# A spectral layer beside softmax attention on one core: two chunks projected together, values stored as rows, the spectral part in two halves of the sequence, seven more buffer pairs and runs of 13 key tiles

## The chip, the core and the metric

The kernel runs on one core of one Trainium2 chip. A core has a matrix engine (TensorE, "PE" in the profile, its weight loads "PEld"), VectorE ("DVE"), ScalarE ("ACT"), GpSimd ("POOL") and SyncE ("SP"), which here issues nearly all DMAs. The on-chip memory SBUF has 128 partitions; matrix products land in PSUM, which has eight banks of 128 x 512 numbers. The metric is the device time of one execution in microseconds (us), the median of several runs.

## What is computed

Two layers work on two inputs of 2048 rows and 448 columns, and their results stand side by side in the output (2048 x 896):

```python
# A: Fourier mixing, the real part alone
a = x @ dft_hid_re.T                        # 2048 x 448
b = x @ dft_hid_im.T
y = dft_seq_re @ a - dft_seq_im @ b         # 2048 x 2048 times 2048 x 448, twice

# B: attention with 16 heads of 28 columns
q, k, v = split(x @ wqkv)
p = softmax(q @ k.T * 28 ** -0.5)           # 2048 x 2048 per head
out = concat_heads(p @ v) @ wo
```

All inputs are 32-bit floats. To keep that precision on TensorE's faster 32-bit format, the kernel splits each factor of the projections and of the spectral part into a high and a low part and multiplies high x high, low x high and high x low. A contraction over 448 rows is 3 x 3 + 2 = 11 matmuls (the last 64 rows hold both parts at once).

## The kernel before, in words

**Stages on TensorE.** The q and k projections (a weight block j of 128 columns, a chunk c of 512 positions, 11 matmuls of 128 x 512 each; seven blocks, four chunks), the values (16 tiles of 128 positions, 11 matmuls of 128 x 448), the spectral part, attention, and the output projection (16 tiles, L1003). Two kinds of work are interleaved over almost the whole span: *attention* (scores, L865, and products with the values, L848) and *fill* (everything else, L581 and L718), which TensorE does between scores, while ScalarE computes exponentials.

**The planner.** The program's instructions are not written in the order in which they run. Each operation is added to `Schedule` with its engine, a *key* (the time at which it is due), an estimated duration, what it depends on, and the buffers that it takes. `Schedule.run` plays the program through with these estimates: when an engine is free it issues the ready operation with the smallest key whose buffers can be had. The order so found is fixed for each engine in the program; the chip then only waits for semaphores. SyncE is one queue, with at most eight DMAs outstanding (`LANES`), whose speed is estimated by `FLOW_IN` in the first 20 us and by `FLOW` later. Fill matmuls form one chain (`last`), each after the one before it; scores form another.

**The head.** The first three weight blocks come as four DMAs of 192 KB (rows k = 0 to 3, L559), x as sixteen of 256 KB (chunk c, rows k, L488). ScalarE writes the high part (L490 for x, L560 for weights), VectorE (L427) or GpSimd (L562) the low one. `first_chunk` takes chunk 0 alone: for each k, three steps (high x high, low weight, low x) of three matmuls each (L616), into three banks. The other chunks go through `project`, 11 matmuls in a row (L581), with two banks in turn (`fill_s`, `NFILL` = 2; the other six banks are `bank_s`). A result goes out through `stored`: ScalarE copies the high part (L597), VectorE subtracts the low part (L598), both are stored to DRAM (L600, L601). `warm` issues `N_WARM` matmuls on a tile of ones before the data are there (L920).

**The values.** A tile of 128 positions is copied to 16 groups of 32 columns (28 of data, a one for the sum, zeros) and stored to `v_d`, laid out head, partition, position tile and column (L675). `head_loads` fetches one head's part for all positions (L773), keyed four planned microseconds before the head begins; two such buffers exist.

**The spectral part.** `hidden(part)` makes a (part 0) or -b (part 1) for all 16 position tiles in `big`, where x lay before, so it waits for the last projection (`x_users`). `sequence(part)` then makes 16 output tiles: four pieces of the sequence matrix for each (a DMA of 256 KB, L523, split by ScalarE, L524, and GpSimd, L530), 12 matmuls per piece (L718), 48 in one bank. In part 0, VectorE copies the result out and it is stored to `y_d` (L732, L733). In part 1, the stored tile is loaded again once piece `Q_YO` has begun (L735), added (L736) and written to the output (L738).

**Attention.** Head h has keys from `begins[h]` = 56 + h x 54.94 us on. `scores` issues for each of its 16 key tiles four matmuls (128 x 512) and four exponentials into two pairs. A *pair* is a buffer of `kept_s`: 128 x 2 x 512 numbers, of which there are `NKEPT` = 22; three more are lent where the memory `wd` is not holding weights. `quad` multiplies a key tile's exponentials by the values: four matmuls that each use 32 columns of the array, side by side. TensorE does such quads in runs: `sums` groups consecutive key tiles, and a run waits for all its exponentials. Its length is taken by `run_size` from the planned time of its first tile: 8 below 230 us, 10 from there on. The planner prices each passage from scores to a run at `PE_TURN`.

**The end.** After a head's last quad, `out_of` fetches the sums, inverts and spreads them by three rounds of DMA, multiplies (GpSimd, L910) and stores the head's output to `on_d`. The output projection reads it in four chunks n, splits it (ScalarE L985; the subtraction on GpSimd for n < `OUT_DVE`, on VectorE from there on), multiplies (L1003) and writes the output (L1011). A flag that sums and values are within bounds decides whether `any_scores`, a slow general path, runs behind; with these inputs it does not.

Of the kernel before, what the change touches and what calls it, by code (L numbers as in the profile page):

```python
# [11 lines left out]
F32 = mybir.dt.float32  # L12
# [8 lines left out]
S = 2048  # L21
# [15 lines left out]
Q_YO = 2  # L37
N_WARM = 7
N_FIRST = 3
RUN_AT = ((0.0, 8), (230.0, 10))  # L40
# [9 lines left out]
OUT_DVE = 2  # L50
# [17 lines left out]
FLOW, FLOW_IN = 200.0, 310.0  # L68
# [264 lines left out]
def tile_kernel(ctx, tc, xa, wre, wim, wd, xb, wqkv, wo, out):  # L333
# [18 lines left out]
    v_d = dram.tile([H, P, NT * VW], F32, name="vd")  # L352
# [5 lines left out]
    big = new("big", [P, 2 * NT * D], F32R)  # L358
# [20 lines left out]
    kept_s.lent = lent  # L379
    fill_s, bank_s = Slots(banks[:NFILL]), Slots(banks[NFILL:])  # L380
# [80 lines left out]

    def x_h(k, s):
        return big[:, k * S + s.start:k * S + s.stop]

    def x_l(k, s):
        return big[:, (3 + k) * S + s.start:(3 + k) * S + s.stop]

    def x_3(s):
        return big[:, 6 * S + s.start:6 * S + s.stop]

    ab_h = big[:, :NT * D].rearrange("p (t d) -> p t d", t=NT)
    ab_l = big[:, NT * D:].rearrange("p (t d) -> p t d", t=NT)
# [113 lines left out]
    def lz(f, *a):  # L586
        return lambda: f(*a)
# [15 lines left out]
    def first_chunk(w):  # L603

        cols = slice(0, CH)
        os = [(bank_s if j else fill_s).slot() for j in range(N_FIRST)]
        pairs = [kept_s.slot() for _ in range(N_FIRST)]
        end = {}
        for k in range(4):
            for step in ((0, 0, 0), (1, 0, 1), (0, 1, 2))[:3 if k < 3 else 2]:  # L610
                wl, xl, n = step
                for j in range(N_FIRST):
                    x = lz(x_3, cols) if k == 3 else lz(x_l if xl else x_h, k, cols)

                    def emit(e, j=j, k=k, n=n, wl=wl, x=x):
                        nc.tensor.matmul(os[j].t, w.part(j, k, wl)(), x(), start=(k == 0 and n == 0), stop=(k == 3 and n == 1))  # L616
                    ready = [*(w.los[k] if wl else w.his[k]), xb_ready[0, k] if xl or k == 3 else xb_hi[0, k]]
                    done = k == 3 and n == 1
                    last[0] = pe(fkey(1, M512), emit, d=M512, deps=[last[0], *ready],
                                 use=[*w.own, os[j], *([pairs[j]] if done else ())])  # L620
                    if done:
                        end[j] = last[0]
# [301 lines left out]
    for c in range(NC):  # L924
        load_x(c, 0.2 + 3 * c)
# [206 lines left out]
```

## Time and profile before

| What | Value |
|---|---|
| median of 3 runs | 1010.89 us (1010.7 to 1011.0) |
| the profiled execution | 1010.71 us, of which the span of the trace 1008.9 us |
| TensorE | 1001.6 us busy, 5634 matmuls |
| its weight loads | 735.3 us |
| ScalarE | 712.3 us |
| GpSimd | 366.9 us |
| VectorE | 319.8 us |
| DMA | 124.84 MB, 109908 packets, 48640 of them under 512 B |
| first matmul on data | 5.28 us from the start of the span |
| granted TensorE clock | 1.000 on average |

The profile's rows give an engine, a line of the kernel, what is written and read (buffer numbers left out), shapes and times. In rows in order of time, the first column is the start, the second the length, "x3" the number of instructions in the group, and the bracket the idle time before it with what ended it. A matmul's length is its passage through the array; consecutive ones overlap, so what one costs is the distance from start to start. The quads appear with two records per matmul, so a run of 8 key tiles has 64 records.

### The profile page before, as it was taken

Reading aid. Unit: us, or ns where it says so; the run is one execution under the profiler, and the core shown is the slowest. Engines: PE = TensorE matmul, PEld = TensorE weight load, DVE = VectorE, ACT = ScalarE, POOL = GpSimd, SP = SyncE. Lnnn points to the kernel's source line nnn. Section 1 sums busy time; section 2 is a strip of 40 time slices with the busy share of each in tenths; the row PEclk is TensorE's granted clock in tenths of the full one; section 3 lists DMA queues with packets and bytes.
Section 4 is the critical chain, followed back from the end, with each engine's and each line's share of the span. In section 5 each row is a group of like instructions: output and inputs, shape, how many; then the busy total and the mean of one; then the engine's idle time right before and its main releaser. Section 6 shows DMA issues by size and latency. Waiting matters only on the chain.

```text
span 1008.9 us, 15993 instructions
## 1 busy us (share of the span) xinstructions
PE 1001.6 (99%) x5634; PEld 735.3 (73%) x5634; DVE 319.8 (32%) x608; ACT 712.3 (71%) x1410; POOL 366.9 (36%) x338
## 2 busy tenths in 40 slices
PE   8999999999999999999999999999999999999998
PEld 7896667777766876686668667766786677667797
DVE  6362525251515042412314051614042152300112
ACT  6117979788767866796679778877786687668242
POOL 5112234353324323442325443434334252444530
PEclk9999999999999999999999999999999999999999
DMA  9797464323233333333233424332433343233463
GB/s 327 226 163 205 127 188 150 98 76 114 69 102 102 112 96 106 97 106 102 80 111 110 132 71 119 93 112 80 148 98 100 117 141 105 70 123 117 139 187 130
DMA packets 109908, 124.84 MB, mean 124 GB/s; under 512 B 48640, under 2 KB 61440, under 8 KB 109824
## 3 DMA queue, kind: packets, MB, share of 16 engines
q1 hardware_dynamic: 109824, 123.78, 40.8%
q8 instruction: 45, 0.74, 0.3%
q14 instruction: 39, 0.32, 0.1%
HBM read 89.92 MB, written 33.69 MB: 123 GB/s over the span
## 4 chain that ended last, share of the span: by engine, by line
PE 98%; DVE 1%; DMA 1%; SPq 0%; issue 0%; DVEq 0%
PE bank L718 31%; PE bank L865 23%; PE bank L848 22%; PE bank L581 17%; PE bank L1003 4%; PE bank L806 1%; DMA kept<-xb 1%; DVE big L427 0%; SPq L488 0%; SPq L559 0%; DVE kept L598 0%; DVE kept L736 0%; DVEq L427 0%
## 5 line engine op out<-in xcount | busy, mean ns | idle before, releaser
L869 ACT ACTIVATE kept<-bank 128x512 f32<-128x512 f32 x944 | 509.4, 673 | 90.7 <-PE bank L865 87.6
L530 POOL TENSOR_TENSOR wlo<-wraw,whi 128x512 fp32r<-128x512 f32 (+1 forms) x164 | 202.9, 1237 | 471.4 <-ACT whi L524 397.1
L865 PE MATMUL bank<-q,k 98*128 98x512 f32 x960 | 329.4, 398 | 0.0
L718 PE MATMUL bank<-big,whi 128*128 128x448 f32 x1024 | 310.9, 367 | 0.0
L848 PE MATMUL bank<-kept,v 128*32 128x512 f32 x2016 | 224.4, 593 | 0.0
L718 PEld LDWEIGHTS bank<-big,whi 128*128 128x128 f32 x1024 | 193.3, 189 | 29.2 <-issue 3.4
L865 PEld LDWEIGHTS bank<-q,k 98*128 98x128 f32 x960 | 180.4, 188 | 44.2 <-issue 11.7
L718 PE MATMUL bank<-big,wlo 128*128 128x448 f32 x512 | 188.3, 368 | 0.0
L848 PEld LDWEIGHTS bank<-kept,v 128*32 128x32 f32 x2016 | 63.5, 110 | 144.4 <-issue 142.3
L524 ACT ACTIVATE whi<-wraw 128x512 fp32r<-128x512 f32 x164 | 113.8, 694 | 21.0 <-PE bank L718 17.0
L718 PEld LDWEIGHTS bank<-big,wlo 128*128 128x128 f32 x512 | 96.7, 189 | 16.9 <-issue 5.9
L837 POOL TENSOR_TENSOR kept<-kept,mb 128x512 f32<-128x512 f32 x54 | 79.5, 1473 | 62.9 <-DVE mb L832 27.5
L581 PE MATMUL bank<-wd,whi 128*128 128x448 f32 x256 | 79.8, 367 | 0.0
L811 DVE STREAM_TRANSPOSE mb<-bank 128x512 f32<-128x512 f32 x64 | 45.8, 715 | 101.6 <-PE bank L806 87.9
L839 ACT ACTIVATE kept<-kept 128x512 f32<-128x512 f32 x64 | 45.1, 772 | 33.3 <-POOL kept L837 29.9
L581 PE MATMUL bank<-big,whi 128*128 128x512 f32 x175 | 60.1, 394 | 0.2 <-DVE kept L598 0.2
L832 DVE STREAM_TRANSPOSE mb<-am 128x512 f32<-128x512 f32 x64 | 45.4, 710 | 41.1 <-POOL kept L837 39.9
L810 ACT ACTIVATE kept<-bank 128x512 f32<-128x512 f32 x64 | 41.6, 672 | 22.5 <-PE bank L806 21.6
L581 PEld LDWEIGHTS bank<-wd,whi 128*128 128x128 f32 x256 | 48.3, 189 | 6.1 <-issue 0.8
L894 ACT ACTIVATE kept<-bank 128x512 f32<-128x512 f32 x16 | 9.5, 597 | 55.1 <-PE bank L848 55.1
L776 DVE TENSOR_REDUCE ok<-v 128x1 f32<-128x512 f32 x16 | 11.0, 686 | 115.5 <-DMA v<-vd 115.4
L736 DVE TENSOR_TENSOR kept<-bank,kept 128x448 f32<-128x448 f32 x15 | 9.3, 623 | 120.2 <-PE bank L718 106.0
(74 smaller groups left out, 745.8 us busy)
## 6 DMA issues: line engine op xcount, KB each, us to landing
wraw<-wre SPq DMA_DIRECT2D x64, 256.0 KB
wraw<-wim SPq DMA_DIRECT2D x64, 256.0 KB
qkd<-kept SPq DMA_DIRECT2D x40, 256.0 KB
wraw<-xa SPq DMA_DIRECT2D x32, 256.0 KB
k<-qkd SPq DMA_DIRECT2D x64, 112.0 KB
q<-qkd SPq DMA_DIRECT2D x64, 112.0 KB
out<-kept SPq DMA_DIRECT2D x31, 224.0 KB
kept<-xb SPq DMA_DIRECT2D x16, 256.0 KB
```

The lines of the kernel that those rows point to most:

```text
L524: a = act(key + (0 if early else 1), lambda: nc.scalar.activation(self.hi.t, raw.t, AF.Copy), ACT_S, soon=SOON, deps=[ld], acq=[self.hi], ...
L530: b = sch.add(e, at, lambda g: eng[g].tensor_tensor(self.lo.t[:, :n], raw.t[:, :n], f32(self.hi.t)[:, :n], op=ALU.subtract), deps=[a], acq ...
L581: nc.tensor.matmul(o.t[:, :cols], w(), x(), start=(i == 0), stop=(i == n - 1))
L718: nc.tensor.matmul(o.t[:, :D], a.t[:, k, :], b[:, q * 4 + k, :], start=(q == 0 and k == 0 and j == 0), stop=(q == 3 and k == 3 and j == 2))
L810: made.append(act(key, lambda o=o, s=s: nc.scalar.activation(s.t, o.t, AF.Copy), deps=[m], use=[o, s.pair], lock=[o]))
L811: t = dve(key, lambda o=o, tm=tm: nc.vector.transpose(tm.t, o.t), 0.73, deps=[m], acq=[tm], use=[o], lock=[o], own=RAW_S)
L832: t = dve(key, lambda mb=mb, c=c: nc.vector.transpose(mb.t, f32(am.t)[:, c * NT:(c + 1) * NT].unsqueeze(2).to_broadcast([P, NT, 32])), 0.7 ...
L837: sh = sch.add({"DVE": 0.8, "POOL": POOL_2}, key, lambda e, s=s, mb=mb: eng[e].tensor_tensor(s.t, s.t, mb.t, op=ALU.add), deps=[t, made[c] ...
L839: shown.append(act(key, lambda s=s: nc.scalar.activation(s.t, s.t, AF.Exp, scale=SCALE), ACT_S, deps=[sh], use=[s.pair]))
L848: nc.tensor.matmul(o.t[c * VW:(c + 1) * VW, :], VT[h].t[:, kt // 4, kt % 4, :], tiles[c].t, start=(kt == 0), stop=(kt == NT - 1))
L865: m = pe(key, lambda e, o=o, q=q, kt=kt: nc.tensor.matmul(o.t, KT[h][kt // 4].t[:KM, kt % 4 * P:(kt % 4 + 1) * P], q.t[:KM, :], start=True ...
L869: es[h, kt].append(act(key - 20, lambda o=o, p=p: nc.scalar.activation(p.t, o.t, AF.Exp, scale=SCALE), deps=[m], use=[o, p.pair]))
```

## The change

Six things change together.

- **Two chunks together.** `first_chunks` takes chunks 0 and 1: for each k it does the nine matmuls of chunk 0, then those of chunk 1, into six banks. x for chunk 1 is now requested between that of chunk 0 and the next weights. Two more warm-up matmuls are issued; the planner's time for the warm-up stays as it was.
- **Values as rows.** `v_d` is laid out partition, position tile, head and column: a tile's store is one contiguous row per partition, a head's load is 16 pieces of 32 numbers per partition.
- **x in two sides.** x lies in two tiles of half the sequence each. The first later takes a and b; the second is given up after the last projection (`held`) and serves as seven more pairs.
- **The spectral part in two halves of the sequence.** `hidden` and `sequence` run four times, for part 0 and 1 and the two halves; a pass sums eight position tiles, 24 matmuls per bank. The first pass stores its tiles, the next two load, add and store them, the last loads, adds and writes the output. The hidden weights are loaded again for each pass, into the memory that is otherwise lent.
- **Runs of 13.** A run has 8 key tiles below 200 planned us and 13 from there on.
- **Smaller settings.** `FLOW` is 225 (was 200), `OUT_DVE` 1 (was 2), `Q_YO` 1 (was 2, of then four pieces, now two).

```diff
-Q_YO = 2
-N_WARM = 7
+Q_YO = 1
+N_WARM = 9
-RUN_AT = ((0.0, 8), (230.0, 10))
+RUN_AT = ((0.0, 8), (200.0, 13))
-OUT_DVE = 2
+OUT_DVE = 1
-FLOW, FLOW_IN = 200.0, 310.0
+FLOW, FLOW_IN = 225.0, 310.0
...
-    v_d = dram.tile([H, P, NT * VW], F32, name="vd")
+    v_d = dram.tile([P, NT, H * VW], F32, name="vd")
...
-    big = new("big", [P, 2 * NT * D], F32R)
+    SIDE = 7 * S // 2
+    xs = [new(f"x{i}", [P, SIDE], F32R) for i in range(2)]
...
+    more, N_MORE = [], SIDE // (2 * CH)
+    def place_of(i):
+        if not more:
+            more.append(sb.tile([P, N_MORE, 2, CH], F32, tag="x1", name="more"))
+        return more[0][:, i]
+    held = [Slot(kept_s) for _ in range(N_MORE)]
+    for i, slot in enumerate(held):
+        slot.i = len(kept_s.tiles)
+        kept_s.tiles.append(lambda i=i: place_of(i))
...
-    def first_chunk(w):
+    def first_chunks(w, chunks):
+        os = {(c, j): (bank_s if j else fill_s).slot() for c in chunks for j in range(N_FIRST)}
+        pairs = {cj: kept_s.slot() for cj in os}
         end = {}
         for k in range(4):
+            for c in chunks:
+                for wl, xl, n in ((0, 0, 0), (1, 0, 1), (0, 1, 2))[:3 if k < 3 else 2]:
+                    for j in range(N_FIRST):
...
-                v_done[c].append(dma(key - 20, lambda vs=vs, c=c, t=t: nc.sync.dma_start(
-                    v_d[:, :, (4 * c + t) * VW:(4 * c + t + 1) * VW].rearrange("h p x -> p h x"),
-                    vs.t.rearrange("p (h x) -> p h x", h=H)), extra=1.0, deps=[b], use=[pair]))
+                v_done[c].append(dma(key - 20, lambda vs=vs, c=c, t=t: nc.sync.dma_start(v_d[:, 4 * c + t, :], vs.t),
+                                     deps=[b], use=[pair]))
...
-    def sequence(part, made):
+    def sequence(part, half, made):
         src = wim if part else wre
+        phase = 2 * part + half
         for tt in range(NT):
...
-            for q in range(4):
+            for q in range(2):
...
-            if part == 0:
+            if phase == 0:
...
-                dma(key, lambda yo=yo, tt=tt: nc.sync.dma_start(out[tt * P:(tt + 1) * P, 0:D], yo.t[:, :D]), deps=[b], use=[pair])
+                to = out[tt * P:(tt + 1) * P, 0:D] if phase == 3 else y_d[tt]
+                y_stored[tt] = dma(key, lambda yo=yo, to=to: nc.sync.dma_start(to, yo.t[:, :D]), deps=[b], use=[pair])
...
-            v.t.rearrange("p c t d -> p (c t d)"), v_d[h]), deps=[d for c in range(NC) for d in v_done[c]], use=[v])]
+            v.t.rearrange("p c t d -> p (c t) d"), v_d[:, :, h * VW:(h + 1) * VW]), extra=1.0, deps=[d for c in range(NC) for d in v_done[c]], use=[v])]
...
-        load_x(c, 0.2 + 3 * c)
+        load_x(c, 0.2 + 3 * c if c > 1 else 0.2 + 0.05 * c)
...
-    first_chunk(w_in)
-    for c in range(1, NC):
+    first_chunks(w_in, (0, 1))
+    for c in range(2, NC):
...
+    for part, half in ((0, 1), (1, 0), (1, 1)):
+        y_last = last[0]
+        key = fkey(0, 0)
+        w_n = Weights(lent)
+        lent.until.append(key - 50)
+        ready = load_w(w_n, lambda k, part=part: wd[:, k, part * D:(part + 1) * D], key - 10, after=[h_last])
+        made = hidden(part, half, w_n, ready, [y_last])
+        h_last = last[0]
+        sequence(part, half, made)
```

More of the change, by code (lines that the diff above doesn't have):

```diff
@@ L609, in first_chunk @@
         for k in range(4):
[L610 to L622, printed above, removed]
@@ L646, in project @@
             own = [hi, lo] if st else [pair]
-            end = chain(key, seq, o, CH, [], w.own if first else [w.hi, w.lo], M512, own, parts)
+            end = chain(key, seq, o, CH, [], w.own if first else [w.hi, w.lo], M512,
+                        [*own, *(held if j == 6 and c == NC - 1 else ())], parts)
             key, out_key = (0.0, 11.0 if j == 0 else 25.0) if first else (key - 10, key - 10)
@@ L665, in values @@
                 key = fkey(11, M448)
-                end = chain(key, seq, o, D, [], [], M448, [pair],
+                end = chain(key, seq, o, D, [], [], M448, [pair, *(held if c == NC - 1 and t == 3 else ())],
                             {3 * k: [xb_ready[c, k], ready[k], *ready[4:][:k // 3]] for k in range(4)}, v_last)
```

64 lines of the change are left out of this document (35 added, 29 removed).

## The prediction

> **What bounds the kernel now.** I read the page first (busy shares and the chain of work that ended last), then TensorE's own waits, then the head in order of time.
>
> ```profile
> span 1008.9 us, 15993 instructions
> PE 1001.6 (99%) x5634; PEld 735.3 (73%) x5634; DVE 319.8 (32%) x608; ACT 712.3 (71%) x1410; POOL 366.9 (36%) x338
> ...
> PE 98%; DVE 1%; DMA 1%; SPq 0%; issue 0%; DVEq 0%
> ```
>
> ```profile
> PE bank L616 <- ACT big L490: 1.7, 2, 1.0
> PE bank L920 <- POOL kept L921: 1.2, 1, 1.2
> PE bank L581 <- DVE kept L598: 0.2, 1, 0.2
> ```
>
> The chain is TensorE for 98% of the span, and the three rows are all the waits TensorE has, every one in the first 20 us. So time can come only from four places: matmuls taken away (the change takes none away: every projection, spectral and attention matmul is still issued), these early waits, what a matmul costs in its surroundings, and the tail after the last matmul.
>
> **The longer runs.** A score matmul fills the whole array, a value matmul (L848) a 32-column strip of it, and four strips work side by side. Passing between the two forms has a price, read here from the order of time on TensorE around a run of 8 key tiles (64 records) and around a run of 10 (80 records):
>
> ```profile
> 93.27 0.40 PE L581 MATMUL bank<-big,whi 128*128 128x512 f32 x1
> 93.60 7.07 PE L848 MATMUL bank<-kept,v 128*32 128x512 f32 x64
> 100.60 0.50 PE L865 MATMUL bank<-q,k 98*128 98x512 f32 x1
> 100.94 0.40 PE L806 MATMUL bank<-q,k 84*128 84x512 f32 x1
> 101.18 0.64 PE L865 MATMUL bank<-q,k 98*128 98x512 f32 x2
> ...
> 283.78 8.79 PE L848 MATMUL bank<-kept,v 128*32 128x512 f32 x80
> 292.50 0.47 PE L718 MATMUL bank<-big,wlo 128*128 128x448 f32 x1
> ```
>
> From start to start the run of 8 holds TensorE for 100.60 - 93.60 = 7.00 us and the run of 10 for 292.50 - 283.78 = 8.72, so a key tile costs (8.72 - 7.00) / 2 = 0.86 us and a run of 8 has 7.00 - 8 x 0.86 = 0.12 left over. The matmul ahead of the run is followed after 93.60 - 93.27 = 0.33 us, where a score matmul is followed after 0.24 (100.94 to 101.18): 0.09 more. The first one behind the run takes 100.94 - 100.60 = 0.34: 0.10 more. One run so costs 0.12 + 0.09 + 0.10 = 0.31 us, however long it is.
>
> How many runs there are follows from the code. Head h begins at 56 + h x 54.94 us of planned time, so key tile n of all 256 stands at 56 + 3.434 n, and a run takes its size from its first tile. Before, tile 48 (220.8) lies under 230 and tile 56 (248.3) above: 7 runs of 8 and 20 of 10, 27 in all. After, tile 40 (193.3) lies under 200 and tile 48 above: 6 runs of 8, then 208 / 13 = 16 runs: 22 in all. Five runs fewer: 5 x 0.31 = **1.6 us saved**. If a longer run cost nothing extra per tile that is the whole effect; the rows of 8 and 10 show nothing that grows with length.
>
> **The head.** These rows show the first chunk and part of the second; first TensorE, then ScalarE.
>
> ```profile
> 5.28 0.96 PE L616 MATMUL bank<-big,whi 128*128 128x512 f32 x3 [0.68 <-ACT big L490]
> 6.08 0.85 PE L616 MATMUL bank<-big,wlo 128*128 128x512 f32 x3
> 6.77 0.84 PE L616 MATMUL bank<-big,whi 128*128 128x512 f32 x3
> ...
> 8.61 0.96 PE L616 MATMUL bank<-big,whi 128*128 128x512 f32 x3 [1.00 <-ACT big L490]
> ...
> 9.41 0.85 PE L616 MATMUL bank<-big,wlo 128*128 128x512 f32 x3
> ...
> 10.10 1.52 PE L616 MATMUL bank<-big,whi 128*128 128x512 f32 x6
> ...
> 11.46 0.84 PE L616 MATMUL bank<-big,wlo 128*128 128x512 f32 x3
> ...
> 18.94 0.39 PE L581 MATMUL bank<-big,wlo 128*128 128x512 f32 x1
> ...
> 19.50 0.73 PE L581 MATMUL bank<-big,whi 128*128 128x512 f32 x2 [0.17 <-DVE kept L598]
> ```
>
> ```profile
> 7.23 0.52 ACT L560 ACTIVATE whi<-kept 128x384 fp32r<-128x384 f32 x1 [2.00 <-DMA kept<-wqkv]
> 7.93 0.63 ACT L490 ACTIVATE big<-kept 128x512 fp32r<-128x512 f32 x1 [0.18 <-DMA kept<-xb]
> ...
> 10.25 3.28 ACT L490 ACTIVATE big<-kept 128x512 fp32r<-128x512 f32 x5
> ```
>
> Undisturbed, six matmuls take 11.46 - 10.10 = 1.36 us, 0.227 each. The nine of k = 0 should be done at 6.77 + 3 x 0.227 = 7.45, but the next begin at 8.61: 1.16 us lost, because the pieces for k = 1 are converted at 7.23 and 7.93 only. Then 9.41 - 8.61 = 0.80 instead of 0.68: 0.12 lost. Later one step takes 19.50 - 18.94 = 0.56 instead of 0.23: 0.33 lost, where j = 2 of chunk 1 waits for a bank that VectorE still reads (two banks rotate there).
>
> After, the input order is w0, x(0,0), x(1,0), w1, x(0,1), x(1,1) and so on (x(c,k)), and TensorE has eighteen matmuls (4.09 us) per k instead of nine. What must land third is x(1,0). In the rows above, 640 KB (192 + 256 + 192) were in at 7.23 and 896 KB at 7.93; after, x(1,0) ends at 704 KB, by interpolation 7.40. A conversion started at 7.93 let a matmul start at 8.61, so 0.68 on: 8.08. The gap becomes 8.08 - 7.45 = 0.63 instead of 1.16, **0.53 saved**. The low half of k = 0's weights is ready by then, so the 0.12 go too. Eighteen matmuls then last to 8.08 + 2.04 = 10.12. x(0,1) ends at 1152 KB; five pieces of 256 KB came through in 3.28 us (0.66 each), so 7.93 + 0.66 = 8.6, usable at 9.3: no wait. Each later k brings 704 KB (1.8 us at this rate) against 4.09 us of matmuls.
>
> At the end six results leave at once, but over six banks; the bank that chunk 2 needs first holds (0, j = 0), finished eight matmuls (1.8 us) before the end, against a ScalarE copy and a VectorE subtraction of about 0.6 and 0.7. The 0.33 go. The margin is half a microsecond; where an x conversion is queued ahead, 0.3 to 0.7 return. Sum of the head: 0.53 + 0.12 + 0.33 = **1.0 saved**. Bounds: everything lost there, 1.6, to a loss of 0.4, should x(1,0) come as late as 7.93 and the bank wait stay at 0.7.
>
> The two further warm-up matmuls (four records) fall into the gap before 5.28:
>
> ```profile
> 1.24 3.36 PE L920 MATMUL bank<-kept 128*128 128x128 f32 x14 [1.24 <-POOL kept L921]
> ```
>
> At 3.36 / 14 = 0.24 us at most per record they end by 1.24 + 18 x 0.24 = 5.56 on that bound, or 5.1 if the last record's own length isn't counted as spacing; so nothing to 0.3 us. I take nothing; 5.28 is set by the data.
>
> **Values as rows.** A value tile's store becomes 128 pieces of 2 KB where it was 2048 of 128 bytes; a head's load becomes 2048 of 128 bytes where it was 128.
>
> ```profile
> 20.00:40.00 20.00, 20.00 (x91) 16.75 (x90) 9.56 (x16) 7.88 (x15) 5.03 (x5) 1.00 0.83 298
> 40.00:60.00 20.00, 20.00 (x99) 18.39 (x98) 8.22 (x31) 0.60 (x1) 0.00 (x0) 1.00 0.87 159
> ...
> 100.00:200.00 100.00, 100.00 (x560) 67.65 (x556) 37.96 (x71) 84.08 (x169) 32.73 (x35) 1.00 0.46 143
> ```
>
> The last two columns are the DMA engines' share and GB/s. With value stores (from 41 us) the same share moves half as much. The stores leave that crowd, TensorE was fully busy in it, so the gain is nothing: only attention can start earlier. The loads cost 256 KB / 159 against 256 / 298, some 0.8 us more each, into a share of 0.46 or less. [...]
>
> **The spectral branch in halves.** Matmuls are equal: 2 x 16 hidden tiles of 11, 128 pieces of 12. Four passes evict 64 tiles instead of 32, and 48 of them add a y tile loaded again: 32 more VectorE operations, 32 more stores and 32 more loads of 224 KB, and eight more weight loads.
>
> ```profile
> L736 DVE TENSOR_TENSOR kept<-bank,kept 128x448 f32<-128x448 f32 x15 | 9.3, 623 | 120.2 <-PE bank L718 106.0
> ...
> yd<-kept SPq DMA_DIRECT2D x16, 224.0 KB
> ...
> DMA packets 109908, 124.84 MB, mean 124 GB/s; under 512 B 48640, under 2 KB 61440, under 8 KB 109824
> ```
>
> 32 x 0.62 = 20 us of VectorE, which is 32% busy; 14.7 MB of y more on 124.8; 72 DMA issues more on SyncE. All lies beside TensorE, so nothing. If that cover were gone, one late eviction would hold one of two banks. Each new pass waits for the previous one's last matmul, but fill matmuls already stand in one order on TensorE, so this adds no idle time; scores lie between. In return the second half of x becomes seven buffers: 29 pairs (before 22, and three lent at times in both), of which a run of 13 holds 26 (before 20 of 22).
>
> **The tail.**
>
> ```profile
> 938.73 23.50 PE bank L718 x115
> 962.23 8.97 PE bank L1003 x44
> ...
> 1003.84 0.83 PE bank L718 x4
> 1004.67 0.02 issue
> 1004.69 0.62 DVE kept L736
> ```
>
> Behind the last run 23.5 us of spectral matmuls cover the way to the output projection, and 4.2 us follow the last matmul (1008.9 - 1004.7). The last run is three tiles longer, but the work moved behind the last score is work taken from before it, and all of TensorE's order comes earlier. I leave the tail as it is, plus or minus 0.5. The subtractions of chunk 1 that go from GpSimd to VectorE shorten a step that is covered already.
>
> **Sum.** 1.6 + 1.0 = 2.6 us off. The profiled execution took 1010.71 (span 1008.9 and 1.8 around it), the median is 1010.89, 0.18 more; 1010.9 - 2.6 = **1008.3**. Differences under 0.2% (2.0 us) count as no change here, about what a measurement of this kernel can tell from none.
>
> **Rivals.** (1) Only the runs help (chance 0.16): the DMA engines share themselves among the queued pieces, x(1,0) lands with the others near 8, and the bank wait stays. For it: the first two pieces allowed a start at 5.28, yet the third came at 7.23. Against: from there the pieces follow in the order of issue. Time 1010.9 - 1.6 = 1009.3. (2) The tail grows (0.10): the last 13 tiles end 3 x 0.86 = 2.6 us later, the covering spectral work has been used up, and the gain is given back: 1010.9 - 2.6 + 2.6 = 1010.9. Against: 23.5 us of cover. (3) Slower: the pairs run out (0.12). A run holds 26 of 29; y tiles now need a pair in three passes of four, for load, add and store (the tail shows 4.2 us from a last matmul to a landed store). When the three spare pairs are taken, an eviction waits, both fill banks stay full, and TensorE idles before each of 16 runs. It decides from 4.6 / 16 = 0.29 us per run; at 1 us per run, 1010.9 - 2.6 + 16 = 1024. Against: before had 2 spare and TensorE never waited. (4) Slower: value loads late (0.05). Each run waits for its head's load; at 0.5 us in 16 runs, 1010.9 - 2.6 + 8 = 1016. Against: 0.8 us more on a load issued some 7 us ahead of the head's first finished tile (4 before it begins, 3.4 for a tile).
>
> **Chances and range.** The forecast has 0.57, all but 0.05 of it faster by over 0.2% (under 1008.9); that 0.05, (1) and (2) are 0.31 within; (3) and (4) 0.17 slower. Low: 1.6 + 1.6 + 0.5 = 3.7 off, 1007.2. High: (1) and (2) inside, 1011.4 with 0.5 of tail; (3) and (4) stay out.
>
> **What would show it.** Right: 22 runs, 16 of them of 104 records and 13 x 0.86 + 0.12 = 11.3 us; the second group of nine near 8.1 us and the 67th projection matmul a microsecond before its 22.14; no TensorE wait after 20 us; 4.2 us of tail. Wrong: TensorE waits on VectorE or DMA between 200 and 940 us, a start of chunk 1 after 8.6, or a hole before the output projection.
>
> ```profile
> 22.14 0.39 PE L581 MATMUL bank<-big,whi 128*128 128x512 f32 x1
> ```

## The result, and the profile after

The changed kernel takes 1013.14 us (median of 13 runs, 1012.62 to 1013.73) beside 1010.86 for the kernel before: a ratio of 1.0024, 95% interval 1.0016 to 1.0031. It is 2.3 us slower, and the forecast was 2.6 faster. The profiled execution took 1012.99 us, with a span of 1011.3.

The page of the changed kernel, first the busy shares, then the chain by engine:

```profile
span 1011.3 us, 16178 instructions
PE 1002.6 (99%) x5638; PEld 735.5 (73%) x5638; DVE 341.0 (34%) x647; ACT 714.2 (71%) x1418; POOL 366.2 (36%) x341
...
PE 96%; DMA 2%; DVE 1%; ACT 0%; issue 0%; SPq 0%
```

TensorE has the work that it had and is as full; VectorE has 21 us more, as forecast. The head, in order of time on TensorE, and ScalarE at the end of it:

```profile
5.01 0.95 PE L633 MATMUL bank<-x,whi 128*128 128x512 f32 x3
5.80 0.86 PE L633 MATMUL bank<-x,wlo 128*128 128x512 f32 x3
6.50 1.78 PE L633 MATMUL bank<-x,whi 128*128 128x512 f32 x6
8.12 0.85 PE L633 MATMUL bank<-x,wlo 128*128 128x512 f32 x3
...
19.69 0.84 PE L633 MATMUL bank<-x,wlo 128*128 128x512 f32 x3
21.35 0.73 PE L598 MATMUL bank<-x,whi 128*128 128x512 f32 x2 [0.81 <-DVE kept L615]
```

```profile
18.49 1.31 ACT L507 ACTIVATE x<-kept 128x512 fp32r<-128x512 f32 x2 [0.16 <-DMA kept<-xb]
19.71 2.04 ACT L614 ACTIVATE kept<-bank 128x512 fp32r<-128x512 f32 x4
```

The six from 6.50 on are the last three of chunk 0 and the first three of chunk 1, nearly without a gap: the second chunk came at 7.31, earlier than forecast (8.1). But the first projection behind the head waits for a bank, 21.35 - 19.69 = 1.66 us for three matmuls that take 0.68, because ScalarE converts x until 19.71 before it reads the first of six results. The 67th projection matmul starts at 21.35 instead of 22.14, 0.79 earlier; 0.27 of that stands at the very start, where the first matmul on data comes at 5.01 instead of 5.28.

A run of 13 from start to start, 264.15 to 275.44, is 11.29 us (forecast 11.3); there are 22 runs, 16 of 104 records:

```profile
264.15 1.06 PE L868 MATMUL bank<-kept,v 128*32 128x512 f32 x8
...
275.44 0.50 PE L885 MATMUL bank<-q,k 98*128 98x512 f32 x1
```

So far all is as forecast. TensorE's waits, of the matmuls and (second fence) of the weight loads ahead of them, tell the first thing that is not; one row of the kernel before stands last.

```profile
PE bank L940 <- POOL kept L941: 1.2, 1, 1.2
PE bank L598 <- DVE kept L615: 0.8, 1, 0.8
PE bank L885 <- ACT kept L889: 0.2, 1, 0.2
```

```profile
PEld bank L885 <- ACT kept L889: 7.1, 31, 0.6
...
PEld bank L885 <- ACT more L889: 1.3, 6, 0.3
```

```profile
PEld bank L865 <- ACT kept L869: 3.8, 20, 0.3
```

Score matmuls wait for a bank that an exponential on ScalarE still reads, 37 times and 8.4 us instead of 20 times and 3.8. Most of such a wait is hidden under the matmul that runs: of the 8.4 us the matmuls themselves show 0.2 (first fence). What TensorE lost I take from start to start: every fill or score matmul behind 36 us that takes at least 15 ns longer than its kind usually does. Before there are 20 such stretches with 0.82 us lost, after there are 38 with 2.97.

The second thing is at the end. The last matmul ends at 1004.96 (1004.66 before), and the span at 1011.32 (1008.88): the tail is 6.36 us instead of 4.22. The rows of SyncE's instructions on the branch over the general path and on the kernel's end say where; after, then before:

```profile
L1050 SPq COMPARE_BRANCH  x2: 38/46/53, 1007.0 to 1007.4; - x2
```

```profile
L1150 SPq EVENT_SEMAPHORE  x14: 17/28/28, 1009.7 to 1011.3; - x14
```

```profile
L1028 SPq COMPARE_BRANCH  x2: 38/46/53, 1006.6 to 1006.7; - x2
```

```profile
L1128 SPq EVENT_SEMAPHORE  x14: 17/28/28, 1007.2 to 1008.8; - x14
```

SyncE comes to the first of its two branch instructions at 1006.95 and to the first instruction behind both at 1009.66, 2.71 us later; before it is 0.59 (1006.64 to 1007.24). In what follows, "the branch" is the first of the two. The instructions behind them are the same ones and take as long. The account of the 2.45 us of span:

| Term | us |
|---|---|
| head (67th projection matmul) | -0.79 |
| five passages into and out of runs, 0.338 each as measured | -1.69 |
| stretches of score and fill matmuls, 2.97 - 0.82 | +2.15 |
| from the last value matmul to the last matmul of all, 66.41 - 65.93 | +0.48 |
| tail | +2.14 |
| left over | +0.16 |

### The profile page after: what moved, and what is told of

The parts are those of the page before. It is cut to its first block, busy times and chain, and to the rows that moved or that the text cites. A ratio compares the mean times of both kernels' runs of the same rounds, so it can differ in the third digit from the quotient of the medians.

```text
span 1011.3 us, 16178 instructions
## 1 busy us (share of the span) xinstructions
PE 1002.6 (99%) x5638; PEld 735.5 (73%) x5638; DVE 341.0 (34%) x647; ACT 714.2 (71%) x1418; POOL 366.2 (36%) x341
## 4 chain that ended last, share of the span: by engine, by line
PE 96%; DMA 2%; DVE 1%; ACT 0%; issue 0%; SPq 0%
PE bank L737 31%; PE bank L885 22%; PE bank L868 22%; PE bank L598 16%; PE bank L1025 4%; PE bank L826 2%; DMA kept<-xb 1%; DMA kept<-wqkv 0%; DVE qm L838 0%; DVE am L841 0%; SPq L505 0%; DVE mb L831 0%; DVE mb L852 0%; DVE kept L857 0%; DVE kept L615 0%
## 5 line engine op out<-in xcount | busy, mean ns | idle before, releaser
L889 ACT ACTIVATE kept<-bank 128x512 f32<-128x512 f32 x732 | 417.5, 713 | 76.3 <-PE bank L885 74.1
L737 PE MATMUL bank<-x,whi 128*128 128x448 f32 x1024 | 312.5, 367 | 0.0
L737 PEld LDWEIGHTS bank<-x,whi 128*128 128x128 f32 x1024 | 193.4, 189 | 27.5 <-issue 1.7
L868 PE MATMUL bank<-kept,v 128*32 128x512 f32 x1580 | 209.0, 593 | 0.0
L737 PE MATMUL bank<-x,wlo 128*128 128x448 f32 x512 | 188.2, 368 | 0.0
L889 ACT ACTIVATE more<-bank 128x512 f32<-128x512 f32 x220 | 130.8, 704 | 9.6 <-PE bank L885 8.7
L737 PEld LDWEIGHTS bank<-x,wlo 128*128 128x128 f32 x512 | 96.7, 189 | 15.3 <-issue 4.2
L868 PE MATMUL bank<-more,v 128*32 128x512 f32 x452 | 87.1, 592 | 0.0
L857 POOL TENSOR_TENSOR kept<-kept,mb 128x512 f32<-128x512 f32 x40 | 59.4, 1485 | 48.1 <-DVE mb L852 29.9
L830 ACT ACTIVATE kept<-bank 128x512 f32<-128x512 f32 x58 | 39.4, 698 | 29.5 <-PE bank L826 29.4
L598 PE MATMUL bank<-x,whi 128*128 128x512 f32 x154 | 52.8, 394 | 0.8 <-DVE kept L615 0.8
```

The source lines that it names most:

```text
L598: nc.tensor.matmul(o.t[:, :cols], w(), x(), start=(i == 0), stop=(i == n - 1))
L737: nc.tensor.matmul(o.t[:, :D], a.t[:, k, :], b[:, q * 4 + k, :], start=(q == 0 and k == 0 and j == 0), stop=(q == 1 and k == 3 and j == 2))
L857: sh = sch.add({"DVE": 0.8, "POOL": POOL_2}, key, lambda e, s=s, mb=mb: eng[e].tensor_tensor(s.t, s.t, mb.t, op=ALU.add), deps=[t, made[c] ...
L868: nc.tensor.matmul(o.t[c * VW:(c + 1) * VW, :], VT[h].t[:, kt // 4, kt % 4, :], tiles[c].t, start=(kt == 0), stop=(kt == NT - 1))
L889: es[h, kt].append(act(key - 20, lambda o=o, p=p: nc.scalar.activation(p.t, o.t, AF.Exp, scale=SCALE), deps=[m], use=[o, p.pair]))
```

## The experiments

Theory F: the jump over the general path waits for code that SyncE hasn't fetched; it depends on where the branch stands in SyncE's program, and has nothing to do with what the change computes. Theory S: the score matmuls wait for ScalarE, which is full in some places, so that what the head and the runs save is partly lost there. The first four runs were made before these were formed. The kernel before, run on the same chip, had 1010.62 us in the first group, 1010.84 in the second, 1010.88 in the third and 1010.47 in the fourth.

### The first four

**e1_runs10**, the changed kernel with the run lengths of the kernel before:

```diff
-RUN_AT = ((0.0, 8), (200.0, 13))
+RUN_AT = ((0.0, 8), (230.0, 10))
```

> The changed kernel with the runs of before: 8 key tiles below 230 planned us, 10 above, so 27 runs instead of 22. Theory A (longer runs pay 0.33 us less per run but let score matmuls wait for ScalarE, because the exponentials of 13 tiles must fit between two runs): the five runs cost 1.7 us, the waits of scores on ScalarE shrink from about 2.4 us to about 0.8 us as in the kernel before, so the last matmul comes within 0.5 us of the changed kernel's 1004.6 us. Rival B (the waits come from the spectral part in halves, whatever the runs): waits stay near 2.4 us and the last matmul comes 1.7 us later, at 1006.3. In both, the time after the last matmul depends on where SyncE's program ends in memory and may be 4.2 or 6.4 us.

1012.97 us, ratio 1.0023 [1.0014, 1.0032]; 27 runs, last matmul 1005.07, tail 6.35, stretches 2.47. Five more passages at 0.338 make 1.69, but the last value matmul came only 0.63 later than in the changed kernel (939.18 and 938.55) and the last matmul of all 0.11. The longer runs are worth next to nothing here, though each passage costs what the forecast said, and the tail has nothing to do with them.

**e2_pad** makes the general path, which isn't executed, longer:

```diff
             nc.gpsimd.dma_start(rd, total[DH:DH + 1, :])
+            for _ in range(48):
+                nc.sync.dma_start(rd, total[DH:DH + 1, :])
```

> The changed kernel with 48 more SyncE transfers in the general path that is jumped over; nothing that is executed changes. Theory A (the 2.1 us that the changed kernel spends more after its last matmul are SyncE's jump over that path, 2.3 us instead of 0.5, and depend on where the target lies in memory): the jump takes another time, 0.4 to 3 us, and the total moves with it, best case 1013.1 - 2 = 1011.1. Rival B (the last transfer itself, or the branch in a longer program, takes longer): 6.4 us after the last matmul as in the changed kernel, 1013.1 in total. TensorE's order and its last matmul at 1004.6 stay in both.

1013.04 us, ratio 1.0024 [1.0014, 1.0033]; from branch to end again 2.71 us, tail 6.35, though SyncE now does eight semaphore instructions between its two branches. That the jump goes further made no difference here. The 67th projection matmul came at 20.45 here instead of 21.35 (the bank wait at the end of the head is not the same in every execution), and the last matmul at 1004.88 instead of 1004.96: of 0.9 us gained early, 0.1 arrived. TensorE has the same matmuls in the same order in both, so they can be compared one by one: the lead of 0.89 is carried unchanged to 780 us and is down to 0.18 at 787. There ScalarE waits for the weights of the next hidden pass, which the halves load again; the changed kernel, then e2:

```profile
778.98 0.58 ACT L525 ACTIVATE wd<-wraw 128x448 fp32r<-128x448 f32 x1 [0.39 <-DMA wraw<-wd]
```

```profile
778.80 0.58 ACT L525 ACTIVATE wd<-wraw 128x448 fp32r<-128x448 f32 x1 [0.81 <-DMA wraw<-wd]
```

The weights are there only 0.18 us earlier, and from then on to 787 us ScalarE goes from conversion to exponential without a pause. e13, below, loses a lead of 0.59 at the same place. Why the weights land no earlier is not shown.

**e3_flow200**, the planner's old estimate of DMA speed:

```diff
-FLOW, FLOW_IN = 225.0, 310.0
+FLOW, FLOW_IN = 200.0, 310.0
```

> The changed kernel with the planner's transfer speed of before (200 instead of 225 GB/s). Theory A (the extra TensorE time is scores waiting on ScalarE in long runs): the waits stay near 2.4 us, last matmul within 0.7 us of 1004.6. Rival C (the plan counts on transfers that come too late): the waits go, last matmul near 1002.5.

1015.59 us, ratio 1.0051 [1.0038, 1.0065]; stretches 6.28. The estimate is not the cause; the new one is the better. One detail served later: here the jump took 2.15 us, neither 0.6 nor 2.7.

**e4_head_only**, the kernel before with the new head:

```diff
-    first_chunk(w_in)
-    for c in range(1, NC):
+    first_chunks(w_in, (0, 1))
+    for c in range(2, NC):
```

> The kernel before with only the head changed: x of chunks 0 and 1 requested in turn, both projected together, nine warm-up matmuls. From the changed kernel's trace: the 67th projection matmul comes at 21.35 instead of 22.14, so 0.8 us earlier; everything behind it as before. Expected 1010.9 - 0.8 = 1010.1. Rival: the head's gain is lost again behind it (a start of attention that does not move), 1010.9.

1010.61 us, ratio 1.0000 [0.9991, 1.0009]. The 67th projection matmul comes 1.41 us earlier (20.73), the 133rd 1.50 (35.83 instead of 37.33), the last matmul of all 0.12. Where it went shows in the waits:

```profile
PEld bank L866 <- POOL q L836: 0.9, 1, 0.9
```

At 74 us a score matmul waits for GpSimd, which is still making q; before 100 us the stretches are 1.05 us instead of 0.04. TensorE is early, its first scores aren't, and it runs into their sources.

### Where the jump's time comes from

In the 18 traces of this case an 8 KB packet of the instruction queue q14 stands within 1.5 us of SyncE's instructions 209, 337, 465 and so on, 81 more than a multiple of 128, in 157 of 172 cases up to the branch; of moments taken at random, 11% have one so near. The changed kernel has 112 more SyncE instructions (1377, before 1265): transfers of y and of weights, and the waits ahead of them. Its branch is the 1359th = 10 x 128 + 79, two short of such a place, from which I infer that the code behind it hadn't been fetched. Two packets stand behind the branch:

```profile
q14 instruction: 2, 0.02, 2.6%
```

(the changed kernel, 1006.5 to 1008.5 us). Two stand there in the kernel before as well (1006.98 and 1007.79), so the packets alone do not tell whether SyncE waits for one. But the branch before is the 1247th = 9 x 128 + 95, 14 us behind instruction 9 x 128 + 81 (992.88, a packet at 992.09), and the place of the branch can be moved.

**e5_after_24** and **e6_before_98** move the branch by small transfers in the changed kernel and in the kernel before:

```diff
+    def with_pads(h, load):
+        load()
+        for i in range(PADS.get(h, 0)):
+            nc.sync.dma_start(spare[h, i], wqkv[:1, 0, :16])
```

> The changed kernel with 21 more transfers of 64 bytes, three behind each value load of seven heads, so that SyncE's last branch stands some 24 instructions further on in its program. Theory F (the jump over the general path waits for its own code): in the traces so far a packet of 8 KB is fetched each time that SyncE has passed 80 more than a multiple of 128 instructions; the changed kernel's branch is its 1359th, one short of such a fetch, and what it jumps to lies 172 further on, two blocks of 128 away. Moved by 24 the branch comes after that fetch: from the first branch to the end's first instruction 0.6 us instead of 2.71, from the last matmul to the end of the span 4.2 us instead of 6.36, time 1010.9, the last matmul where it was (1004.9 within 0.5). Rival G (the tail grew for what the engines still have to do, or with the number of SyncE's instructions): 6.3 us or more and 1013.1.

> The kernel before with 98 more transfers of 64 bytes on SyncE, 14 behind each value load of seven heads; nothing else of it is changed. Theory F: its last branch goes from the 1247th to about the 1346th instruction of SyncE, 13 short of the next fetch, as in the changed kernel: jump 2.7 us, tail 6.3 us instead of 4.2, time 1012.8 to 1013.2 though not one step of the change is in it. Rival G (the tail belongs to what the change computes at the end): 4.2 us, 1010.7. If the transfers themselves held something up, stretches of TensorE would grow beyond the 0.8 us of the kernel before.

e5: 1011.28 us, ratio 1.0004 [0.9995, 1.0013]; branch to end 0.59, tail 4.23. e6: the kernel before now has the long tail:

```profile
L1036 SPq COMPARE_BRANCH  x2: 38/46/53, 1070.0 to 1070.0; - x2
```

```profile
L1136 SPq EVENT_SEMAPHORE  x14: 17/28/28, 1072.7 to 1074.3; - x14
```

2.75 us and a tail of 6.39, without one step of the change. Both ways the jump's time came as F said, and G falls. The forecast of e6's time was badly off: 1074.79 us, ratio 1.0627 [1.0612, 1.0643]. SyncE needs 0.59 us to issue one of these transfers, 14 in a row hold up the loads behind them, and TensorE stands still six times for 5 to 13 us; stretches are 64.2 us. In e5, seven times three in a row cost 1.2 us at the last matmul (1006.15).

**e9_after_14** put 14 of them where SyncE waits anyway:

> The changed kernel with 14 transfers of 64 bytes on SyncE in front of the last head's fetch of its sums, where SyncE waits for 10 us anyway (928.5 to 939.2 in the trace of e7_dve_high). The 21 of e5 stood behind value loads, and the last matmul came 1.2 us later than in the changed kernel. Theory F (the jump waits for code that is not yet fetched): tail 4.2, and now the last matmul where the changed kernel has it, 1004.96 within 0.3: time 1010.8 within 0.3, level with the kernel before. Rival: the last matmul stays at 1006.1, so that the shift of the program itself costs TensorE time, and 1011.3 comes again.

1015.19 us, ratio 1.0039 [1.0026, 1.0052]; tail 4.25, last matmul 1009.81. The jump is short again, but the 10 us weren't free: the transfers took 9.67 us in a row, and loads behind them came late (below). **e13_after_12** put 12 behind the first twelve stores of output rows, where no weights are left to load:

```diff
-                dma(key, lambda oo=oo, r0=r0: nc.sync.dma_start(out[r0:r0 + P, D:], oo.t[:, :D]), deps=[e], use=[pair])
+                def rows_out(oo=oo, r0=r0, c=c, at=2 * i + t):
+                    nc.sync.dma_start(out[r0:r0 + P, D:], oo.t[:, :D])
+                    if c < 3:
+                        nc.sync.dma_start(spare[4 * c + at], wqkv[:1, 0, :16])
+                dma(key, rows_out, deps=[e], use=[pair])
```

> The changed kernel with 12 transfers of 64 bytes on SyncE, one behind each of the first twelve stores of output rows, where no weights are left to load. Theory F: the last matmul stays at 1004.96 within 0.3, the tail is 4.25 instead of 6.36, time 1010.9 within 0.3: the fetch of code is the whole of the tail. Rival: any time above 1011.5 means that a part of the 2.1 us is not the fetch.

1010.80 us, ratio 1.0003 [0.9995, 1.0012]; last matmul 1004.94, tail 4.23. The last matmul stayed, and 2.3 us are back: the jump is the whole of what the tail had grown by. Jump and tail, by the number of the branch:

| Kernel | number of SyncE's branch, less 10 x 128 (before: 9 x 128) | branch to end, us | tail, us |
|---|---|---|---|
| before | 95 | 0.59 | 4.22 |
| e6_before_98 | 66 | 2.75 | 6.39 |
| e1_runs10 | 74 | 2.71 | 6.35 |
| changed kernel, e2_pad | 79 | 2.71 | 6.36, 6.35 |
| e3_flow200 | 82 | 2.15 | 6.03 |
| e13_after_12 | 91 | 0.60 | 4.23 |
| e5_after_24 | 103 | 0.59 | 4.23 |

In the ten other kernels, counted likewise, the branch stands at 88 to 107 and the jump takes 0.59 to 0.60 us. e3's branch (1009.91) came 0.1 us behind instruction 10 x 128 + 81, with a packet at 1009.97, 0.06 us behind the branch. That the place of the branch decides is shown, both ways: at 66 to 79 the jump takes 2.71 to 2.75 us, at 88 to 107 it takes 0.59 to 0.60. That SyncE waits there for code is inferred from the step at 81 and the packets; no row shows the wait itself. The price is 2.71 - 0.59 = 2.1 us.

### Where the savings went

**e7_dve_high** is e5 with the high parts of the hidden pass on VectorE, **e10_dve_14** the same on e9 and **e14_dve_12** on e13. The line of part 0 is shown; the negating copies of the other part move likewise. In the traces these are 32 copies, 24 us of ScalarE's time; the 104 of the expectations is wrong.

```diff
-                a = act(key - 10, lambda o=o, hi=hi: nc.scalar.activation(hi, o.t[:, :D], AF.Copy), 0.43, soon=SOON, deps=[end, *after], use=[o])
+                a = dve(key - 10, lambda o=o, hi=hi: nc.vector.tensor_copy(hi, o.t[:, :D]), 0.54, soon=SOON, deps=[end, *after], use=[o])
```

> The kernel of e5 with the 104 high parts of the hidden pass copied from PSUM by VectorE instead of ScalarE. Theory S (the matmuls' 2.8 us are score matmuls that wait for a bank because ScalarE is full while the hidden passes run: one exponential and one copy in 2.25 us of fill): those waits shrink from 3.0 us to under 1.5, the last matmul ends 1.5 to 2.5 us sooner, at 1002.5 to 1003.5, and the time is 1008.5 to 1009.5 if the tail is 4.2. Rival V (VectorE is as full there, or the waits come from elsewhere, the first tiles' adds above all): the last matmul within 0.5 of e5's, the waits as long.

> The kernel of e9 with the 104 high parts of the hidden pass copied by VectorE instead of ScalarE. Theory S (score matmuls wait for ScalarE, which is full in the hidden passes): against e9 the last matmul 1.3 us sooner, as e7 was against e5, at 1003.6, with the stretches behind score matmuls down from 3.0 us to 1.7 or less; time 1009.5 or less. Rival V (the gain in e7 came out of the stalls that its transfers had made): last matmul within 0.4 of e9's.

> The kernel of e13 with the 104 high parts of the hidden pass copied by VectorE. In e10 against e9 the stretches of TensorE before 900 us fell from 4.3 to 1.4 us. Theory S: here from 3.0 to about 1.0, last matmul 1003.0 to 1003.7, time 1008.9 to 1009.6, faster than the kernel before by 0.13 to 0.2%. Rival V: last matmul 1004.6 or later, 1010.6.

| Pair | last matmul | stretches | time and ratio |
|---|---|---|---|
| e5, e7 | 1006.15, 1004.83 | 4.54, 3.87 | e7 1009.33, 0.9986 [0.9977, 0.9996] |
| e9, e10 | 1009.81, 1008.62 | 4.3, 1.4 (before 900 us) | e10 1013.72, 1.0027 [1.0019, 1.0036] |
| e13, e14 | 1004.94, 1002.97 | 3.48, 1.93 | e14 1009.09, 0.9985 [0.9977, 0.9994] |

In the clean pair the waits of e13, then of e14:

```profile
PEld bank L885 <- ACT kept L889: 7.7, 35, 0.6
PEld bank L885 <- ACT more L889: 1.7, 7, 0.4
```

```profile
PEld bank L885 <- ACT kept L889: 5.1, 23, 0.6
```

Each time the last matmul of the profiled execution came 1.2 to 2.0 us sooner, and the median time 1.5 to 2.0, with nothing edited but the engine of these copies (the planner then orders a few others differently). In the clean pair the stretches account for 1.55 of the 1.97. S holds in sign and place: the stretches near 400, 600 and 830 us went, those where first tiles or late weights hold ScalarE up (329 and 785 us) stayed, so that e7's and e14's waits fell less than I had said. e14 is faster than both kernels, by 1.4 us (0.15%) than the one before: its interval excludes no change, but the prediction counts differences under 0.2% as none.

**e12_before_dve** moves the same copies in the kernel before:

> The kernel before with the high parts of its 104 hidden blocks copied by VectorE instead of ScalarE, nothing of the change. Theory S: its score matmuls wait 0.8 us in all, so there is next to nothing to gain: last matmul 1004.2 to 1004.7, time 1010.2 to 1010.7. Rival: the gain of 1.3 us in e7 has nothing to do with the halves: last matmul 1003.4 and 1009.4.

1010.89 us, ratio 1.0001 [0.9992, 1.0010]; last matmul 1004.68, stretches 0.56 (the profiled execution's tail was 5.2, 1 us of it SyncE's wait for another engine at the end). In the kernel before, whose stretches lose 0.82 us, moving the copies brought nothing.

**e16_dve_runs10** is e14 with the runs of 8 and 10:

> The kernel of e14 with the runs of 8 and 10 tiles of the kernel before (27 instead of 22) and 16 transfers instead of 12. Theory S: with the copies off ScalarE the longer runs are worth what their turns cost, 5 times 0.34: last matmul 1.2 to 1.8 us behind e14's, time 1010.3 to 1011.3. Rival A (whatever is saved is taken back by the next wait): last matmul within 0.5 of e14's, as e1 was to the changed kernel (0.11).

1012.07 us, ratio 1.0018 [1.0009, 1.0026]; last matmul 1004.87, 1.90 behind e14's. That is a little over S's figure, but not for its reason alone. At the last value matmul e16 is 1.05 behind (passages 1.69, stretches before 900 us 0.70 less), and 0.85 come after it. There the output projection loses 1.3 us at 983 us, because a conversion on ScalarE waits 2.12 us for a load; the loads of that group are issued 1.2 us later than e14's, right behind one of the four transfers that e16 has more. Without that stall e16 would be some 0.6 us behind e14 (an estimate, 1.90 - 1.3). Like for like, at the last value matmul, the shorter runs cost 0.63 in e1 and 1.05 in e16. So the run does not decide between S and its rival, and that moving the copies makes longer runs worth more is not shown. The tail of 5.4 here, and of 5.2 in e15, ends with the last y store's landing, 3.5 us after its issue; the jump is short in both.

### The rest of the change alone

**e8_rows_only**, the kernel before with the values as rows:

```diff
-    v_d = dram.tile([H, P, NT * VW], F32, name="vd")
+    v_d = dram.tile([P, NT, H * VW], F32, name="vd")
```

> The kernel before with the values stored as rows and nothing else of the change. Prediction's term: 0 (all beside TensorE): 1010.6 within 0.4, last matmul at 1004.66 within 0.3, tail 4.2. Rival D: the store's or the load's descriptors are shorter by row and land later, some score or PV matmul waits: over 1011.2.

1010.59 us, ratio 0.9998 [0.9989, 1.0007]; last matmul 1004.65, tail 4.21. Nothing, as forecast.

**e11_halves_14** and **e15_halves_12** keep of the change the halves, the pairs, the rows and the smaller settings, with the transfers of e9 and of e13; runs and head are those of the kernel before (the head's edit is shown in part):

```diff
-    first_chunks(w_in, (0, 1))
-    for c in range(2, NC):
+    first_chunk(w_in)
+    for c in range(1, NC):
```

> Of the change the halves, the seven more pairs and the value rows only: the first chunk and the runs of 8 and 10 tiles are those of the kernel before; the 14 transfers of e9 keep the jump short. Theory H (the halves cost what the head and the longer runs bring): nothing is saved, so the cost stands bare: the 67th projection matmul near 22.1 as before, last matmul 2 to 3 us behind the kernel before's 1004.66, at 1006.5 to 1007.5, time 1012.5 to 1013.5. Rival A (the head's gain is absorbed wherever score matmuls wait, as in the head alone, so it never reached the end and the halves cost the less): last matmul 1004.7 to 1005.4, as with runs of 10 and the new head (1005.07), time 1010.6 to 1011.3.

> Of the change the halves, the seven more pairs and the value rows only (first chunk and runs of 8 and 10 as in the kernel before), with the 12 transfers of e13. Theory H: the head's and the runs' savings did arrive and the halves cost as much: last matmul 1006.5 to 1007.5, time 1012.5 to 1013.5. Rival A: savings before a wait for ScalarE are absorbed by it, so that the halves without them end at 1004.7 to 1005.4, time 1010.7 to 1011.3.

e11: 1018.43 us, ratio 1.0073 [1.0060, 1.0086], most of it the transfers' own stall near 950 us (stretches 6.84 of 10.28), so it tells nothing of the halves. e15: 1013.14 us, ratio 1.0022 [1.0014, 1.0031], 0.9 of it the landing of that last store; last matmul 1006.42, stretches 2.59. Its runs spread from 1010.49 to 1015.05; the profiled execution has the median time. In it the last matmul is 1.76 us behind the kernel before's and the stretches are 1.77 longer: the halves, with the settings that came with them, cost 1.8 us, a little less than H said and far more than A. The largest shows how; TensorE, then ScalarE of e15:

```profile
829.05 0.37 PE L736 MATMUL bank<-x,whi 128*128 128x448 f32 x1
829.99 0.50 PE L884 MATMUL bank<-q,k 98*128 98x512 f32 x1 [0.57 <-ACT more L888]
```

```profile
828.82 0.63 ACT L541 ACTIVATE whi<-wraw 128x512 fp32r<-128x512 f32 x1 [0.75 <-DMA wraw<-wim]
829.36 1.07 ACT L888 ACTIVATE more<-bank 128x512 f32<-128x512 f32 x2
830.31 0.63 ACT L858 ACTIVATE more<-more 128x512 f32<-128x512 f32 x1
830.83 0.60 ACT L888 ACTIVATE more<-bank 128x512 f32<-128x512 f32 x1
```

ScalarE stands in order behind a conversion whose weights land 0.75 us late; behind it exponentials start every 0.5 us without a pause, and the score matmul that needs their bank waits.

## Why the prediction was wrong

- **The tail, "as it is, plus or minus 0.5": this step failed and turned the sign.** It grew by 2.14 us. I had looked at the work that could stand behind the last matmul and not at the program; "72 DMA issues more on SyncE" were priced as issues, at nothing, but the 112 instructions more put the branch at 79 instead of 95, and the jump took 2.71 us instead of 0.59. With the tail as forecast the kernel takes 1010.8 (e13): no difference, still not 1008.3.
- **The halves, "all lies beside TensorE, so nothing": failed too, 1.8 us.** The extra VectorE work does lie beside it, and no fill matmul waits for an eviction or a pair. What I did not price is ScalarE, whose 71% I had before me: score matmuls need a bank every time, and where ScalarE is held up by a late load (779 us, and 829 us in e15) or has the hidden pass's copies as well, it has no slack to catch up. The reading "all the waits TensorE has" left out its weight loads: the kernel before already has 20 waits of theirs for ScalarE, 3.8 us, and 0.82 us lost in such stretches.
- **The runs, 1.6: the size was right (1.69), the step from it to the end was not.** Of it 0.63 is left at the last value matmul and 0.11 at the last matmul (e1): e1's stretches are 0.50 shorter than with runs of 13, its head came 0.42 earlier, and the matmuls behind its last run take 0.52 less. "The rows of 8 and 10 show nothing that grows with length" looked at the runs alone.
- **The head, 1.0: 0.79 in the profiled execution, made up otherwise.** In the eleven other kernels with this head the 67th matmul comes 1.0 to 1.7 us before 22.14, so the size was about right. The gap ahead of chunk 1 went almost wholly, more than the 0.53; of the bank wait, "the 0.33 go", the opposite came, 0.98 lost. My own proviso covered it: an x conversion queued ahead returns 0.3 to 0.7. Most of what is gained is taken back further on (e4: 0.12 of 1.41 arrives; e2: a lead of 0.89 is lost at 780 to 787 us).
- **Values as rows, 0: right (e8, ratio 0.9998).** The packets under 512 B are as many with the rows (48640 in both traces), and no time moved. The 0.8 us for each load was an estimate from the rates with and without the value stores.
- **Rivals.** (1) fell: x(1,0) came in its order. (2) had a larger tail but by late output work, which didn't happen. (3) and (4) fell: no fill matmul waits for a pair, no value matmul for a load. The slower outcome came by a way that none of the four named.

Not settled are the 0.48 us more between the last value matmul and the end of the matmuls, which the kernels with runs of 13 have (66.41 in the changed kernel, e13 and e14) and those with shorter ones don't (65.9 in before, e1 and e15), and 0.16 of the account. The 0.48 lie in the first 120 matmuls there: 24.90 us from start to start instead of 24.42, at a granted clock of 1.00 in both, while those behind them take 41.21 in both. What makes each of them 4 ns longer is open.

## What to carry to other kernels

In this case a saving on the busiest engine was worth what the next engine could follow (the head: 0.12 of 1.41 us arrived in e4): before adding up what TensorE gains, look at the stage's second engine (here ScalarE at 71% on average, full in places), and if gains vanish, take work off that one (24 us of copies moved: the last matmul 1.2 to 2.0 us sooner). Where two runs have the same instructions in the same order, their difference matmul by matmul shows the place at which a lead is lost. When a small change moves the time by about 2 us and the last matmul hasn't moved, compare the tail instruction by instruction: the branch near the end took 0.59 or 2.71 us here, by how many instructions stand before it on SyncE, and edits that add some flipped it both ways (e5, e6).

## What the runs showed of the hardware

The price of the jump, 2.1 us by the place of the branch, is above. Beside it, e9 and e10 show what followed a pause of TensorE. e9 pauses 2.3 us, e10 3.4:

```profile
952.70 0.65 PE L737 MATMUL bank<-x,whi 128*128 128x448 f32 x2 [2.32 <-DVE kept L755]
```

```profile
950.48 1.08 PE L737 MATMUL bank<-x,whi 128*128 128x448 f32 x2 [3.41 <-DVE more L755]
951.36 0.57 PE L737 MATMUL bank<-x,wlo 128*128 128x448 f32 x1
951.73 0.95 PE L737 MATMUL bank<-x,whi 128*128 128x448 f32 x2
```

The granted clock, the third column from the end, in the stretches behind them, e9's first:

```profile
953.00:957.00 4.00, 4.00 (x21) 3.72 (x20) 1.58 (x11) 0.11 (x1) 1.29 (x1) 1.00 0.77 207
```

```profile
950.50:956.00 5.50, 5.50 (x15) 4.89 (x16) 3.34 (x12) 1.11 (x2) 1.72 (x2) 0.50 0.65 190
957.00:963.00 6.00, 6.00 (x31) 5.57 (x30) 0.62 (x1) 1.26 (x2) 4.82 (x4) 1.00 0.73 228
```

Behind the shorter pause TensorE goes on at full clock (1.00); behind the longer one the clock is 0.50 and matmuls come every 0.37 us instead of 0.20 for 5.5 us. That stall so cost some 2.5 us more than itself (an estimate, 15 matmuls at 0.17 more). Averaged over the span the granted clock is 0.996 in e10, 0.997 in e11, which pauses 3.44 us, and 0.971 in e6 with its six pauses; in every other profiled execution of this case it is 0.999 or 1.000. In e10 the half clock is granted from 949.17 us on (0.83 on average over 946.7 to 950.4), 2.1 us after the last matmul ended, and e9's pause of 2.32 us shows none: from which length of pause on it comes, these runs do not show.
